# Delta-rule attention and a gated FFN on one core: the state product over two heads at once with a block-diagonal state, solve and within as stacked pairs of batch elements, and a new dealt order

## The chip, the cores and the metric

The kernel runs on one core of a Trainium2 chip. The metric is the device time of one execution in microseconds (us); the time shown for a kernel is the median of several runs. The names of the engines are those of the profile: PE (TensorE, matrix products; PEld are its weight loads), DVE (VectorE), ACT (ScalarE), POOL (GpSimd), SP (SyncE, which issues most DMAs).

## The reference

A delta-rule recurrence over 768 time steps for 4 batch elements and 8 heads of width 48, then a feed-forward layer with the gate h * cos(h). All data are 32-bit floats.

```python
k_n = k / (np.linalg.norm(k, axis=-1, keepdims=True) + 1e-06)
state = np.zeros((B, H, D, D))                       # B, H, S, D = 4, 8, 768, 48
for t in range(S):
    kt, vt, bt = k_n[:, :, t], v[:, :, t], beta[:, :, t, None]
    y[:, :, t] = np.einsum('bhd,bhde->bhe', q[:, :, t], state)
    v_old = np.einsum('bhde,bhd->bhe', state, kt)
    state = state + bt[:, :, :, None] * np.einsum('bhd,bhe->bhde', kt, vt - v_old)
x = y.transpose(0, 2, 1, 3).reshape(B * S, H * D)    # 3072 x 384
h = x @ w_in                                         # 384 x 2048
out = (h * np.cos(h)) @ w_out                        # 2048 x 384
```

## The kernel before

**Units.** Time is cut into 24 units of C = 32 steps. In a unit, 4 batch elements of 32 steps fill the 128 partitions: a quarter is 32 partitions (one batch element), a half is 64. Two units together are 256 tokens, one step of the feed-forward layer. Within a unit the recurrence is solved in closed form, by these stages (the numbers are lines of the kernel):

1. `turn` and `turn_out` (583 to 602), from unit 8 `load_blocks` and `turn_blocks` (356, 603): the keys and queries are transposed into kq_t, with the 48 features of an even head on partitions 0 to 47 and of an odd head on 64 to 111.
2. `gram` (609): for each of 4 head pairs j, 4 batch elements b and 2 parities `par` of the head a matmul of the keys with keys and queries, 48 rows, 32 columns of the array, 64 moving columns. `gram_keys` and `gram_queries` (627, 740) scale and mask the results on DVE.
3. The triangular inverse: units 0 to 3 by rows on PE, DVE and POOL (643 to 738); from unit 4 the gram goes to DRAM (`gram_put`, 749), comes back in another layout (`gram_get`, 764), is inverted on POOL column by column (`invert_eye` 774, `invert` 778: lines 791 and 798), and goes back through DRAM (`put` 800, `get` 806) into a tile zt.
4. `through_state` (816): keys (a = 0) and queries (a = 1) of the unit times the state, 64 matmuls of 48 rows, 32 columns of the array and 48 moving columns. The result p_kq lies in PSUM, batch elements on quarters, the parity of the head in the bank.
5. `right_side` (837, DVE): v less the keys' product. `solve` (882): the inverse times that, 32 matmuls of 32 by 32 with 48 moving columns; units 0 to 3 have two more products of that shape first (`solve_half`, `between`, by way of `triangular`, 850).
6. `solve_out` (895, DVE): weighs the result by beta and spreads it over two slots, one for each batch element of a half (the other slot is zero). `update` (908): 16 matmuls of 64 by 64 with 96 moving columns add to the state; `update_out` (920, DVE) adds them to the tile st.
7. `within` (926): the masked query gram times u adds to the queries' product in p_kq, 32 matmuls of 32 by 32, 48 columns. `within_out` (940, ACT) copies the sum to y, `features` (944) transposes y by three full transposes, `features_out` (954, ACT) copies the result into the features x of the feed-forward layer.

From unit 8 (PLAIN_TURNS) the odd heads are kept with the two halves of the partitions swapped: `home` (294) says in which quarter a batch element lies. The k loads (336), `gram`, `gram_put`, `weigh` (565), `spread_beta_home` (425), `solve`, `update` and `within` follow it.

**The feed-forward layer.** `hidden` (966) is a plain product for the first 256 tokens; later steps form the products by a scheme with 20 instead of 24 block products for the first layer (`layer`, 1145) and 7 instead of 8 for the second (`product`, 1225), with sums of operands on DVE and POOL. In between, ACT and DVE compute cos and the gate. The weights are loaded in 28 pieces (`narrows`, 458) and rewritten on ACT, DVE and POOL.

**The order.** Each stage is a task with dependences (`unit`, 1333). Which task is emitted when is written out by hand in one long list (`Order.LINE`), a table `Order.OTHER` names the tasks that run on their second engine or queue. Each engine works through its instructions in that order. So a stage that waits on PE holds all that PE has behind it. Buffers are counted in `Order.run`: PSUM has two banks for `p_kq`, two for `two` (turns, gram, solve, update, features), three for `h`, and one for the output.

Of the kernel before, what the change touches and what calls it, by code (L numbers as in the profile page):

```python
# [24 lines left out]
def _consts():  # L25

    p = np.arange(128)
    share = p // 64
    row = SPLIT * np.arange(C // SPLIT)[None, :] + share[:, None]
    return np.concatenate(
        [
            np.eye(128),
            p[:, None] % C < np.arange(C)[None, :],
            p[:, None] // C % 2 == np.arange(2)[None, :],
            p[:, None] // 16 % 2 == np.arange(2)[None, :],  # L40
            (row[:, :, None] == np.arange(C)).reshape(128, -1),
        ],
        axis=1,
    ).astype(np.float32)


class Order:

    OTHER = {
        ('weigh', 0, 0), ('fold', 0), ('unfold', 0), ('weigh', 0, 1), ('fold', 1), ('unfold', 1),  # L50
        ('fold', 2), ('fold', 3), ('unfold', 2), ('unfold', 3), ('in_sums', 6), ('in_sums', 8),
        ('in_sums', 14), ('in_sums', 15), ('x_sum', 2, 'd'), ('x_sum', 2, 'n'), ('x_sum', 2, 'm'),
        ('x_sum', 2, 'e'), ('x_sum', 2, 'k'), ('x_sum', 2, 'g'), ('x_sum', 2, 'i'),
        ('x_sum', 2, 'l'), ('x_sum', 2, 'f'), ('x_sum', 2, 'h'), ('x_sum', 2, 'b0'),
        ('left', 2, 1, 0), ('left', 2, 2, 0), ('left', 2, 3, 1), ('x_sum', 3, 'd'),
        ('x_sum', 3, 'n'), ('x_sum', 3, 'm'), ('x_sum', 3, 'e'), ('x_sum', 3, 'k'),
        ('x_sum', 3, 'g'), ('x_sum', 3, 'i'), ('x_sum', 3, 'l'), ('x_sum', 3, 'h'),
        ('x_sum', 3, 'b0'), ('left', 3, 1, 0), ('left', 3, 4, 0), ('x_sum', 4, 'd'),
        ('x_sum', 4, 'n'), ('x_sum', 4, 'm'), ('x_sum', 4, 'e'), ('x_sum', 4, 'k'),
        ('x_sum', 4, 'l'), ('x_sum', 4, 'f'), ('x_sum', 4, 'h'), ('x_sum', 4, 'b0'),  # L60
        ('left', 4, 4, 0), ('left', 4, 3, 0), ('left', 4, 3, 1), ('x_sum', 5, 'd'),
        ('x_sum', 5, 'n'), ('x_sum', 5, 'k'), ('x_sum', 5, 'g'), ('x_sum', 5, 'b0'),
        ('left', 5, 1, 1), ('left', 5, 4, 0), ('left', 5, 3, 0), ('left', 5, 3, 1),
        ('x_sum', 6, 'd'), ('x_sum', 6, 'n'), ('x_sum', 6, 'k'), ('x_sum', 6, 'g'),
        ('left', 6, 1, 0), ('left', 6, 2, 0), ('left', 6, 2, 1), ('left', 6, 4, 1),
        ('left', 6, 3, 0), ('x_sum', 7, 'd'), ('x_sum', 7, 'n'), ('x_sum', 7, 'm'),
        ('x_sum', 7, 'l'), ('x_sum', 7, 'h'), ('x_sum', 7, 'b0'), ('left', 7, 1, 0),
        ('left', 7, 3, 0), ('x_sum', 8, 'd'), ('x_sum', 8, 'n'), ('x_sum', 8, 'm'),
        ('x_sum', 8, 'g'), ('x_sum', 8, 'l'), ('x_sum', 8, 'h'), ('x_sum', 8, 'b0'),
        ('x_sum', 9, 'd'), ('x_sum', 9, 'f'), ('left', 9, 1, 0), ('left', 9, 2, 0),  # L70
        ('left', 9, 1, 1), ('left', 9, 4, 0), ('left', 9, 4, 1), ('left', 9, 3, 0),
        ('left', 9, 3, 1), ('x_sum', 10, 'd'), ('x_sum', 10, 'n'), ('x_sum', 10, 'm'),
        ('x_sum', 10, 'g'), ('x_sum', 10, 'i'), ('x_sum', 10, 'l'), ('x_sum', 10, 'b0'),
        ('left', 10, 1, 0), ('left', 10, 2, 1), ('left', 10, 3, 0), ('x_sum', 11, 'd'),
        ('x_sum', 11, 'n'), ('x_sum', 11, 'f'), ('x_sum', 11, 'h'), ('left', 11, 1, 0),
        ('left', 11, 4, 0), ('left', 11, 4, 1), ('left', 11, 3, 0), ('left', 11, 3, 1),
# [3 lines left out]
2031 0 1 9 10 2 3 15 16 17 11 54 55 18 56 57 21 4 60 22 23 19 58 61 62 6 24 25 26 27 28 30 34 63 64  # L80
29 93 92 101 65 66 32 102 31 2032 2035 2036 73 95 33 35 36 37 14 123 39 20 40 96 97 2037 2039 2038
124 2033 2034 38 132 133 69 2040 2041 41 67 42 43 44 2043 2044 45 2045 126 127 182 2047 2048 46 47
49 50 2049 2050 68 2042 128 2046 48 181 190 191 71 51 52 70 78 2051 53 98 2055 2056 2052 72 103 104
105 129 207 184 59 185 186 2053 2059 2060 94 2063 208 106 7 107 108 2067 238 2071 75 134 135 2054
739 74 137 138 2064 139 140 141 142 237 144 76 79 77 136 147 143 145 146 740 2075 2065 2061 80 81
82 263 83 148 2057 2068 2062 744 745 2058 741 742 100 84 85 2079 150 151 743 99 2076 86 87 149 2066
152 153 154 88 89 210 211 156 159 90 91 157 264 8 2083 293 240 5 12 109 2069 187 192 2077 193 194
2087 155 160 746 110 162 2072 2073 158 161 163 759 747 241 212 213 195 214 749 748 164 165 111 2084
2085 2080 2081 760 761 112 215 217 113 114 2078 2074 125 2070 2091 762 763 2088 166 2089 769 770
771 115 116 242 774 750 772 773 2082 216 2086 2090 218 117 119 243 244 219 775 776 777 751 778 120  # L90
2092 118 2095 2096 2099 2103 2093 764 246 247 2097 130 167 131 168 752 753 121 183 2107 2094 779
765 766 2100 122 767 220 221 2101 768 2098 2104 2105 209 189 2102 2108 2109 2106 2110 169 807 2111
170 171 172 13 808 822 823 824 173 809 810 174 811 222 2112 2113 2115 2119 319 817 2123 239 175 177
780 818 819 2127 791 176 2116 820 821 178 179 180 295 795 2117 2124 2125 796 265 812 813 814 266
2120 267 188 2131 827 2121 825 826 248 249 815 816 245 250 828 223 251 829 2114 2135 197 224 225
2132 2128 2129 2118 296 830 831 754 755 756 268 269 2136 2130 879 270 2126 2122 757 758 837 838 271
273 198 842 832 781 297 839 840 2139 2140 2133 2137 843 2134 2138 196 199 2141 2142 782 783 272 302
349 322 274 301 226 880 841 833 200 201 203 204 878 298 844 845 202 882 846 894 834 835 803 303 375
358 784 321 357 881 897 883 785 786 227 228 205 206 787 836 229 799 800 788 351 789 804 230 231 888
889 891 232 233 234 848 352 847 235 236 900 901 275 276 902 903 910 904 906 850 853 911 912 854 915  # L100
916 905 913 914 405 790 792 323 793 794 304 305 306 277 907 908 909 307 253 797 856 858 895 919 801
324 325 327 851 326 885 917 278 279 280 281 920 884 849 928 929 918 926 921 892 859 932 852 802 886
890 933 798 860 861 328 922 927 930 805 862 864 923 893 931 252 254 255 329 934 359 936 256 257 259
924 925 899 935 938 937 942 954 258 260 261 262 865 939 958 943 283 887 896 898 940 866 863 284 944
941 945 867 378 431 282 285 946 948 377 461 413 294 320 806 959 286 955 950 855 949 947 353 354 857
287 289 868 869 288 952 960 961 355 953 956 957 414 870 290 291 407 292 1014 330 331 1013 332 871
872 333 334 335 1015 1020 360 361 362 363 966 967 873 1024 1028 336 379 962 963 951 1016 1017 1019
1021 1018 874 875 876 350 380 381 383 309 1025 1026 964 982 968 969 965 985 1029 970 1030 408 978
979 1027 988 1032 299 1031 1039 1023 1033 971 1022 1041 300 310 382 972 973 983 1040 980 1034 337
385 1035 981 1036 1037 1042 1043 1044 984 989 991 993 1045 384 308 311 338 376 434 974 975 1046 312  # L110
487 1038 1047 1049 976 1048 1050 994 977 986 1051 1052 1071 987 1055 1056 313 315 314 995 1053 415
1057 316 339 317 318 992 1054 1072 996 997 433 990 340 435 470 877 490 517 341 342 1075 1058 1073
1074 999 1063 469 1001 343 345 344 1076 409 386 387 388 389 390 391 392 1002 346 1067 1061 1068 410
347 348 1062 1064 1126 1133 1003 416 417 418 406 419 1004 411 1059 1060 1065 1066 1128 1129 1127
998 1130 1131 1132 1136 1134 436 437 439 1000 1005 1006 1069 1137 1141 1007 1009 365 463 1070 393
1138 1091 1139 1010 464 465 1142 1143 438 1140 441 1144 1077 440 442 443 1135 1145 1146 364 1008
356 366 394 471 526 432 543 1078 1092 1011 1096 1152 1147 1153 1079 1080 367 368 1154 1081 1082
1093 1094 1156 1157 1155 1095 1148 1149 369 370 1150 371 372 1151 573 1083 1158 1159 1084 1098 373
1160 395 1087 1088 374 1101 1102 1089 1097 396 397 1162 462 1012 488 1161 1085 1164 398 399 401 402
489 525 599 1163 1168 466 1104 400 1086 1165 1166 1090 1106 1184 1099 1167 444 445 446 1169 403 404  # L120
# [95 lines left out]
def kernel(  # L216
# [73 lines left out]

    def home(n, b, par):
        return quarter(b ^ 2 if n >= PLAIN_TURNS and par else b)

    def by_parity(t):
        return t.rearrange("p (j a) i -> p a j i", a=2)

    bq = ffn_pool.tile([128, NU, C], FP, name="bq", tag="g", bufs=GATES)  # L300
    nc.vector.memset(bq, 0.0)

# [33 lines left out]
    def load(n, what="kqv", eng=(nc.sync,) * B):  # L336
# [4 lines left out]
        for x in what:  # L341
# [5 lines left out]
            if x == "k" and n >= PLAIN_TURNS:  # L347
                parts = [slice(0, H, 2), slice(1, H, 2)]
# [1457 lines left out]
```

## Time and profile before

| | |
|---|---|
| median of 3 runs | 651.01 us (650.0 to 652.37) |
| the profiled execution | 656.79 us, its span 654.2 us |
| mean granted clock of PE | 0.981 |
| PE busy | 619.1 us, 12306 matmul rows |
| DVE, ACT, POOL busy | 505.7, 265.5, 451.1 us |
| state (L828), all rows | 2944 in 23 units |
| solve (L891), update (L914), within (L931) | 1536, 736, 1536 rows |
| features (L950) | 72 rows |

The span is the time from the first to the last instruction; the execution's own time has 2.6 us around it. A row of PE is given with the rows and columns of the array that it uses (48*32), the shape of its moving operand (48x48), and how often it comes. Busy time overlaps where small matmuls run beside each other, so what a stage takes is read from the starts in the timeline.

### The profile page before, as it was taken

To read this page: it belongs to the slowest core of one execution; us is meant where nothing else is said; L and a number is where in the kernel's file an instruction comes from. 1 tells how busy PE (TensorE), PEld (TensorE's weight loads), DVE (VectorE), ACT (ScalarE), POOL (GpSimd) and SP (SyncE) were. 2 spreads that over 40 slices of the span, in tenths; PEclk is the share of its full clock that TensorE was granted. 3 is DMA by queue.
4 is the path that set the end of the run, shared out by engine and by line. 5 is a ranking of instruction groups with operands and counts; after the bars stand their busy time and mean duration, and the time that the engine had idled before them with its cause. 6 is when DMAs were issued, how large, how long until landed. Compare 5 with 4: busy or idle time off the path is not lost.

```text
span 654.2 us, 28227 instructions
## 1 busy us (share of the span) xinstructions
PE 619.1 (95%) x12306; PEld 579.8 (89%) x12306; DVE 505.7 (77%) x948; ACT 265.5 (41%) x469; POOL 451.1 (69%) x788
## 2 busy tenths in 40 slices
PE   5879799999999999998899999999999999999996
PEld 4778798976989999898799999999999999999996
DVE  7789798878999979776787877777777668667681
ACT  3545575731224523611542533622534523435340
POOL 3348989978988888686788986697787584143103
PEclk9979899999999999999799999999999999999999
DMA  7882573555444554434415434423400403000001
GB/s 157 192 217 72 130 217 82 118 107 75 90 68 67 115 73 71 95 67 81 77 29 93 67 62 77 90 40 62 85 7 13 105 4 60 13 2 25 2 13 36
DMA packets 202623, 49.99 MB, mean 76 GB/s; under 512 B 194244, under 2 KB 197460, under 8 KB 202500
## 3 DMA queue, kind: packets, MB, share of 16 engines
q1 hardware_dynamic: 201236, 47.81, 38.0%
q8 instruction: 96, 1.57, 1.0%
q10 hardware_dynamic: 1088, 0.20, 0.2%
q0 software_dynamic: 176, 0.18, 0.1%
q14 instruction: 27, 0.22, 0.1%
HBM read 38.19 MB, written 9.96 MB: 74 GB/s over the span
## 4 chain that ended last, share of the span: by engine, by line
PE 72%; POOL 8%; DVE 7%; DMA 6%; issue 3%; SPq 2%; ACT 2%; DVEq 0%; ACTq 0%; POOLq 0%
PE p_out L1229 23%; PE p_h L1149 23%; PE p_h L971 7%; PE p_out L1172 3%; DMA out_dram<-o 3%; PE p_kq L828 3%; PE p_u L891 2%; PE p_s L914 2%; POOL z L798 2%; POOL part L791 2%; PE p_kq L931 2%; PE p_g L619 2%; DVE turns L1019 1%; DMA qp<-in_q_dram 1%; PE p_z L950 1%
## 5 line engine op out<-in xcount | busy, mean ns | idle before, releaser
L791 POOL TENSOR_TENSOR part<-z,gb 128x126 f32<-128x126 f32 (+22 forms) x310 | 139.4, 450 | 56.2 <-DMA gb<-g_dr 15.7
L798 POOL TENSOR_TENSOR z<-z,part 128x126 f32<-128x126 f32 (+22 forms) x310 | 140.5, 453 | 24.4
L1229 PE MATMUL p_out<-w_out,g_ffn 128*128 128x192 f32 x672 | 122.5, 332 | 1.5 <-DVE o L1281 1.5
L1229 PEld LDWEIGHTS p_out<-w_out,g_ffn 128*128 128x128 f32 x672 | 109.0, 192 | 3.0 <-issue 1.1
L1028 ACT ACTIVATE turns<-turns,halfpi 128x512 f32<-128x512 f32 x96 | 68.7, 721 | 75.4 <-DVE turns L1019 74.8
L1229 PE MATMUL p_out<-w_sum,g_ffn 128*128 128x192 f32 x496 | 89.6, 329 | 1.8 <-DVE o L1281 1.8
L1245 POOL TENSOR_TENSOR g_ffn<-g_ffn 128x512 f32<-128x512 f32 x34 | 46.6, 1380 | 62.1 <-DVE g_ffn L1031 31.8
L1149 PE MATMUL p_h<-x_sum,w_in 128*128 128x128 f32 x640 | 84.8, 279 | 0.7 <-DVE g_ffn L1166 0.7
L1229 PEld LDWEIGHTS p_out<-w_sum,g_ffn 128*128 128x128 f32 x496 | 79.6, 191 | 2.9 <-DVE o L1281 2.2
L1149 PEld LDWEIGHTS p_h<-x_sum,w_in 128*128 128x128 f32 x640 | 78.7, 193 | 2.7 <-DVE g_ffn L1166 1.5
L1012 ACT ACTIVATE turns<-g_ffn,quarter_turn 128x512 int32<-128x512 f32 x70 | 50.0, 720 | 48.4 <-DVE g_ffn L1166 32.6
L1166 DVE TENSOR_TENSOR g_ffn<-g_ffn,p_h 128x512 f32<-128x512 f32 x80 | 54.2, 680 | 14.7 <-PE p_h L1149 12.1
L1019 DVE SCALAR_TENSOR_TENSOR turns<-g_ffn,turns 128x512 f32<-128x512 f32 x70 | 57.6, 831 | 8.6 <-ACT turns L1012 8.5
L1031 DVE TENSOR_TENSOR g_ffn<-turns,g_ffn 128x512 f32<-128x512 f32 x70 | 52.6, 758 | 12.7 <-ACT turns L1028 12.7
L1281 DVE SCALAR_TENSOR_TENSOR o<-p_out,o 128x192 f32<-128x192 f32 x74 | 25.1, 352 | 39.8 <-PE p_out L1229 29.7
L1149 PE MATMUL p_h<-x_sum,in_sum 128*128 128x128 f32 x400 | 54.2, 280 | 1.1 <-ACT p_h L1161 0.6
L971 PE MATMUL p_h<-x_ffn,w_in 128*128 128x128 f32 x384 | 50.4, 293 | 1.5 <-ACT row_copies L712 1.5
L1149 PEld LDWEIGHTS p_h<-x_sum,in_sum 128*128 128x128 f32 x400 | 49.2, 192 | 2.3 <-ACT p_h L1161 0.8
L971 PEld LDWEIGHTS p_h<-x_ffn,w_in 128*128 128x128 f32 x384 | 47.9, 206 | 2.5 <-ACT row_copies L712 1.6
L535 POOL TENSOR_TENSOR knrm<-ksum,halves 128x16 f32<-128x16 f32 (+1 forms) x14 | 37.0, 2646 | 15.7 <-DVE ksum L523 9.0
L1245 DVE TENSOR_TENSOR g_ffn<-g_ffn 128x512 f32<-128x512 f32 x54 | 42.5, 789 | 0.9 <-POOL part L791 0.3
L1149 PE MATMUL p_h<-x_ffn,w_in 128*128 128x128 f32 x320 | 42.8, 277 | 0.0
(144 smaller groups left out, 1041.5 us busy)
## 6 DMA issues: line engine op xcount, KB each, us to landing
gb<-g_dr SPq DMA_DIRECT2D x20, 256.0 KB
vp<-in_v_dram SPq DMA_DIRECT2D x96, 48.0 KB
in_sum<-in_moe_w_out_dram SPq DMA_DIRECT2D x12, 384.0 KB
out_dram<-o SPq DMA_DIRECT2D x23, 192.0 KB
in_sum<-in_moe_w_in_dram SPq DMA_DIRECT2D x8, 512.0 KB
kp<-in_k_dram SPq DMA_DIRECT2D x128, 24.0 KB
z_dr<-z SPq DMA_DIRECT2D x10, 256.0 KB
zt<-z_dr SPq DMA_DIRECT2D x80, 32.0 KB
```

Of the source, the lines that this page charges most:

```text
L535: nc.gpsimd.tensor_tensor(out=scales[m][2][:, part], in0=sums[m, part.start][:, 0:n], in1=halves[:, 0:n], op=ALU.pow,)
L791: nc.gpsimd.tensor_tensor(out=part, in0=z[:, 0:rows, j, None].to_broadcast(shape), in1=a[:, j, None, j + 1 :].to_broadcast(shape), op=ALU. ...
L798: nc.gpsimd.tensor_tensor(out=behind, in0=behind, in1=part, op=ALU.subtract)
L971: nc.tensor.matmul(p_h[:, i], w_in[:, t, (4 * k + i) * 128 : (4 * k + i + 1) * 128], xts[p][:, t, unit * 128 : (unit + 1) * 128], start=(i ...
L1012: nc.scalar.activation(turns[p, f], hidden_of(p, f), AF.Identity, bias=quarter_turn, scale=TURN)
L1019: nc.vector.scalar_tensor_tensor(out=r, in0=hidden_of(p, f), scalar=TURN, in1=t, op0=ALU.mult, op1=ALU.subtract,)
L1028: nc.scalar.activation(r, r, AF.Sin, bias=halfpi, scale=2.0 * math.pi)
L1031: nc.vector.tensor_tensor(out=place(p, f), in0=step_of(rests.pop((p, f)), f), in1=step_of(hidden_of(p, f), f), op=ALU.mult,)
L1149: nc.tensor.matmul(p_h[:, e], in_block(*w)[:, e], x_of(p, b), start=new and e == 0, stop=True, skip_group_check=True,)
L1166: nc.vector.tensor_tensor(out=part_of(p, to), in0=part_of(p, one), in1=part_of(p, two), op=op)
L1229: nc.tensor.matmul(p_o, left(p, part, a)[:, e % 4], right(e, b), start=(e == 0), stop=(e == FT // 2 - 1), skip_group_check=True,)
L1245: either(("left", p, x, s), nc.vector, nc.gpsimd).tensor_tensor(out=left(p, s, to), in0=left(p, s, one), in1=left(p, s, two), op=op)
```

## The change

The state is kept a second time as a tile st_wide, in which each pair of heads is a block-diagonal 128-row matrix (zero elsewhere); two copies a unit (`widen`, ACT or DVE) write the two diagonal blocks. A matmul of `through_state` then takes both heads of a pair: 128 rows, 32 columns, 96 moving columns, 32 matmuls in place of 64. zt becomes one tile that is set to zero once, with a batch element's inverse in its own slot, so that `solve` takes a half of the partitions at a time: 64 by 64, 48 moving columns, 16 matmuls in place of 32 (from unit 4). `within` takes a half of the rows and both slots of u: 16 matmuls with 96 columns. Its result has another layout (quarter 2*jh + i, slot x, then heads), `features` becomes 12 matmuls of 64 by 64 with the identity, and the rows of w_in are loaded to match, in two pieces each. The swapped quarters are gone, and with them the doubled k loads, the two extra puts, the copies in `weigh` and `spread_beta_home`; `weigh` may run on POOL in all units. There are three key buffers in place of four. The start of the inverse is written by three ACT copies of constants, and not copied from a constant loaded by DMA. `Order.LINE` and `Order.OTHER` are new throughout.

```diff
-    def home(n, b, par):
-        return quarter(b ^ 2 if n >= PLAIN_TURNS and par else b)
...
-    kps = [const.tile([128, 2, H, DP], FP, name=f"kp{i}") for i in range(4)]
+    kps = [const.tile([128, 2, H, DP], FP, name=f"kp{i}") for i in range(3)]
...
+    st_wide = const.tile([128, 2, NP, 2, 2, D], FP, name="st_wide")
+    wide_zt = const.tile([128, H, 2, C], FP, name="zt")
+    for t in [wide_zt, st_wide]:
+        nc.gpsimd.memset(t, 0.0)
...
     def invert_eye(m):
         zs[m] = work.tile([128, ROWS, C], FP, name="z", bufs=ZS)
-        nc.scalar.copy(zs[m], eye)
+        z = zs[m].rearrange("p r i -> p (r i)")
+        nc.scalar.copy(z, zero_one[:, 0:1].to_broadcast([128, ROWS * C]))
+        for i in range(SPLIT):
+            ones = z[half(i), i : ROWS * C : SPLIT * (ROWS + 1)]
+            nc.scalar.copy(ones, zero_one[half(i), 1:2].to_broadcast([DP, ROWS]))
...
     def get(n):
-        zts[n] = work.tile([128, H, C], FP, name="zt")
+        zts[n] = wide_zt
         z_dr = z_drs[n // 2].rearrange("r s u h b i -> u b (r s) h i")[n % 2]
         for b in range(B):
-            queue("get", n).dma_start(out=zts[n][quarter(b)], in_=z_dr[b])
+            queue("get", n).dma_start(out=zts[n][quarter(b), :, b % 2], in_=z_dr[b])
...
     def through_state(n):
...
         for a in range(2):
             for j in range(NP):
                 for b in range(B):
-                    for par in range(2):
-                        nc.tensor.matmul(
-                            p_kq[quarter(b), par, a, j],
-                            kq_t[rows48(par), a, b * NP + j],
-                            st[rows48(par), b // 2, j, b % 2],
...
+                    i, x = b // 2, b % 2
+                    if a == 0:
+                        to = p_kq[quarter(b), 0, 2 * j * D : 2 * (j + 1) * D]
+                        begin = j == 0
+                    else:
+                        at = (2 * x + j % 2) * 2 * D
+                        to = p_kq[quarter(2 * (j // 2) + i), 1, at : at + 2 * D]
+                        begin = j % 2 == 0 and x == 0
+                    nc.tensor.matmul(
+                        to,
+                        kq_t[:, a, b * NP + j],
+                        st_wide[:, i, j, x].rearrange("p q e -> p (q e)"),
...
     def solve(n):
...
+                for i in range(2):
                     nc.tensor.matmul(
-                        p_u[home(n, b, par), par, j], zt[quarter(b), h], rhs[quarter(b), h]
+                        p_u[half(i), par, j],
+                        zt[half(i), h].rearrange("p x i -> p (x i)"),
+                        rhs[half(i), h],
                     )
...
+    def widen(n, par):
+        to = st_wide[half(par), :, :, :, par].rearrange("p i j x e -> p (i j x) e")
+        by = st[half(par)].rearrange("p i j x e -> p (i j x) e")
+        if ("widen", n, par) in Order.OTHER:
+            nc.vector.tensor_copy(to, by)
+        else:
+            nc.scalar.copy(to, by)
...
     def within(n):
         u, tt, p_kq = us.pop(n), grams.pop(n), p_kqs[n]
...
+        for jl in range(2):
             for par in range(2):
+                for jh in range(2):
+                    for i in range(2):
+                        h = 2 * (2 * jh + jl) + par
+                        at = (2 * jl + par) * D
+                        nc.tensor.matmul(
+                            out_at[quarter(2 * jh + i), :, at : at + D],
+                            tt[half(i), h],
+                            u[half(i), h],
...
     def features(n):
...
-        for t in range(KT):
-            nc.tensor.transpose(p_z[:, t], y_f[:, t * 128 : (t + 1) * 128], ident)
+        for k in range(KT):
+            for x in range(2):
+                for jh in range(2):
+                    nc.tensor.matmul(
+                        p_z[half(jh), k, x],
+                        y[half(jh), x, k * DP : (k + 1) * DP],
+                        ident[half(jh), half(jh)],
...
-            add(("get", n), "SP", 1.9, lambda: get(n), [("put", m)],
+            add(("get", n), "SP", 1.9, lambda: get(n),
+                [("put", m)] + ([("solve", n - 1)] if n > 2 * ROWED else []),
...
+        state = [("widen", n - 1, i) for i in range(2)]
         add(("state", n), "PE", 1.17 if n else 0.0, lambda: through_state(n),
-            [("gram", n), ("update_out", n - 1)] if n else [("gram_queries", 1)],
+            [("gram", n)] + state if n else [("gram_queries", 1)],
```

## The prediction

> **What bounds the kernel now.** I read the page's busy rows first, then its chain of work that ended last, then who PE waited for, then PE's timeline around three units of the recurrence.
>
> ```profile
> PE 619.1 (95%) x12306; PEld 579.8 (89%) x12306; DVE 505.7 (77%) x948; ACT 265.5 (41%) x469; POOL 451.1 (69%) x788
> PE 72%; POOL 8%; DVE 7%; DMA 6%; issue 3%; SPq 2%; ACT 2%; DVEq 0%; ACTq 0%; POOLq 0%
> ```
>
> PE is busy 95% of the span and carries 72% of the chain; no other engine is over 77%. The waits listed for PE add up to some 30 us, over half of it in the first 75 us; the largest later piece is 4.8 us before the solve at 313.6 us. So, after the first 75 us, what a stage takes on PE is what the end pays. The next lines show these stages (start, time to the modelled end of the last one, count). I take as a stage's cost the distance from its start to the start of the next row, since the modelled ends overlap.
>
> ```profile
> 321.52 1.47 PE L1229 MATMUL p_out<-w_out,g_ffn 128*128 128x192 f32 x8
> 322.82 1.05 PE L1149 MATMUL p_h<-x_sum,w_in 128*128 128x128 f32 x8
> 323.81 1.38 PE L828 MATMUL p_kq<-st,kq_t 48*32 48x48 f32 x128
> 325.12 1.16 PE L1149 MATMUL p_h<-x_sum,in_sum 128*128 128x128 f32 x8
> 326.11 0.49 PE L950 MATMUL p_z<-consts,y 128*128 128x128 f32 x3
> 326.44 1.05 PE L1149 MATMUL p_h<-x_sum,in_sum 128*128 128x128 f32 x8
> 327.33 1.06 PE L1149 MATMUL p_h<-x_ffn,w_in 128*128 128x128 f32 x8
> 328.32 0.80 PE L891 MATMUL p_u<-rhs,zt 32*32 32x48 f32 x64
> 329.05 1.16 PE L1149 MATMUL p_h<-x_ffn,in_sum 128*128 128x128 f32 x8
> 330.04 1.06 PE L1149 MATMUL p_h<-x_sum,w_in 128*128 128x128 f32 x8
> 331.03 0.89 PE L914 MATMUL p_s<-u,kp 64*64 64x96 f32 x32
> 331.85 0.80 PE L931 MATMUL p_kq<-u,tt 32*32 32x48 f32 x64
> 332.58 1.16 PE L1149 MATMUL p_h<-x_sum,in_sum 128*128 128x128 f32 x8
> ```
>
> State 1.31 us, features 0.33, solve 0.73, update 0.82, within 0.73. A matmul is two rows of the trace (32 matmuls of solve are x64), I call a row a pass; a transpose is one. In the large stages a pass of 192 columns costs 1.30/8 = 0.163 us and one of 128 columns 0.89/8 = 0.111: it goes by its columns. By that, 96 columns are 0.081, 64 are 0.056, 48 are 0.041. Small matmuls run beside each other. Unit 2 shows it, from the time before the quarters were swapped:
>
> ```profile
> 81.58 0.88 PE L858 MATMUL p_v<-u_half,halves_z 32*32 32x48 f32 x64 [0.60 <-ACT u_half L868]
> 82.39 2.95 PE L971 MATMUL p_h<-x_ffn,w_in 128*128 128x128 f32 x24
> 85.27 0.88 PE L891 MATMUL p_u<-u_half,halves_z 32*32 32x48 f32 x64
> 86.08 2.95 PE L971 MATMUL p_h<-x_ffn,w_in 128*128 128x128 f32 x24
> ```
>
> Here a batch's rows meet the same quarter of columns, four places in the array, 64/4 = 16 passes each: 16 x 0.041 = 0.66, measured 0.81, so 0.15 is start and drain. Update has four places (two halves by two halves), 8 passes each: 8 x 0.081 = 0.65, measured 0.82, so 0.17. Both fit one rule: **passes per place x columns, plus 0.16 us**; the number of instructions (64 and 32) doesn't enter. From unit 8 on, the swapped quarters give solve and within eight places, and both fall from 0.81 to 0.73.
>
> **The change on PE, stage by stage.**
> - Solve, units 4 to 23: 16 matmuls of 64 by 64, 48 columns, 32 passes on only two places (half to same half): 16 x 0.041 + 0.16 = 0.82. Half the instructions, no gain: +0.09 in 16 units (8 to 23), nothing in 4 to 7. **+1.4 us.**
> - Within: 16 matmuls, 96 columns, 32 passes on four places: 8 x 0.081 + 0.16 = 0.81, as update. +0.08 in 16 units. **+1.3 us.**
> - Features: three transposes of full size (three passes, 0.33) become 12 matmuls with the identity, 24 passes of 64 columns, on two places (half jh to half jh): 12 x 0.056 + 0.16 = 0.83. **+0.50 x 24 = +12.0 us.** No row shows a 64-column matmul of this kind; from below, 24 passes at the rate per pass of today's state (1.31/128 = 0.010) would be 0.25, from above one after the other 24 x 0.056 + 0.16 = 1.5. I take 0.83, by the update row, which is nearest in shape.
> - State, 23 units: 64 matmuls on eight places become 32 with all 128 rows, 32 columns of array and 96 moving columns: 64 passes on four places, the column quarters. If all four always run, 16 x 0.081 + 0.16 = 1.46. But the query half (a = 1) writes quarters 2(j//2)+i: pairs j = 0, 1 use quarters 0 and 1 alone, j = 2, 3 quarters 2 and 3. Then it is 8 passes deep for the keys and 8 + 8 for the queries: 24 x 0.081 + 0.16 = 2.10. The far ends: 64 passes at 0.010 give 0.65; one after the other they take 64 x 0.081 + 0.16 = 5.3. That quarters sharing their rows run together is shown by today's state (two halves of rows, four quarters on each: 64 passes of 0.041 on each half would be 2.6 us in turn, and it takes 1.31). How far PE reaches past a blocked quarter is shown by these two lines, a gram followed at once by a state:
>
> ```profile
> 290.81 0.22 PE L828 MATMUL p_kq<-st,kq_t 48*32 48x48 f32 x1
> 290.82 0.27 PE L619 MATMUL p_g<-kq_t 48*32 48x64 f32 x4
> ```
>
> One pass of state starts ahead of gram's last four, so it reaches some four passes; to start quarters 2 and 3 early it would have to reach past 16. I take 2.10: +0.79 x 23 = **+18.2 us**, and keep 1.46 and 5.3. The Trainium skill, "TensorE: Matmul & The Clock Gate", Part 3 (The mechanism), says that matmuls start in strict program order and only weight loads are pulled ahead. By that rule the state would be near the 2.10 too; the two lines above show that it isn't quite strict here.
> - Gram: as it was, 0.79 alone. Where a state is its neighbour (12 places by the order of before) they share a shape and gram costs 0.58 (290.23 to 290.81); the new state has another shape. **+0.2 x 12 = +2.4 us.**
>
> Sum on PE: 1.4 + 1.3 + 12.0 + 18.2 + 2.4 = +35.3 us. Units 0 to 3 run before 95 us, where PE is idle for some 18 us of the first 100; their share (3 x 0.79 + 4 x 0.50 = 4.4) I count by half: **+33 us**.
>
> **What lies beside PE.** Widen copies 64 rows of 768 elements twice a unit (29 on ACT, 17 on DVE). ACT's square of 128x768 takes 0.84 us, its copy of 128x512 0.62, DVE's add of 128x768 0.95. So ACT gets 29 x 0.84 = 24 us more at 41% busy; DVE gets up to 16 and loses 24 copies of some 0.24 and, with weigh moved to POOL, 7 times 0.96. Neither becomes the bound. But widen is a new wait of state, and behind state all of PE is queued. Today the shortest time from the end of the sum to state is 1.8 us. In the new order at least 3.4 us of PE work (by the costs above) stands between the start of update and the next state, but for one early unit with 2.0; update 0.82, sum 0.95, and one or two widens (0.84 or 1.7) with hand-overs of 0.1 to 0.2 make 2.8 to 3.7. So I cost it at nothing beyond 1 to 2 us; with that cover gone it is at most one widen a unit, 23 x 0.84 = 19 us. The single zt buffer lets get start only after solve of the unit before; 10 us of PE work or more lie between two solves, and four gets take 2.1 us of SP to issue. The fewer DMAs (k loads 8 to 4 a unit, puts 3 to 1; weights 12 more) relieve SP, which isn't late on PE's rows except once. The two more ACT copies of invert's start, the memsets and kps 4 to 3 are hidden behind the same slack. The order dealt anew may save or add some of the 30 us of waits: 0 taken, 8 either way.
>
> So the profiled execution (656.8 us, span 654.2) would become 690; the median of the runs shown, 651.0, lies 5.8 lower, and I forecast 651 + 33 = **684 us**.
>
> **Rivals.**
> 1. All four quarters run in the query half: state 1.46, sum 20.6, less 2: 651 + 18.5 = 670 us. For: in update all four places work at once. Against: the query half names only two quarters for 16 passes. It decides where PE reaches 16 passes ahead. Chance 0.32.
> 2. **Faster: cost goes by the number of instructions.** If every pass costs the 0.010 of today's state, state is 0.65 (-15 us), solve and within 0.33 (-18), features 0.25 (-2): 651 - 35 = 616. It decides where the pass is shorter than the issue of the places' passes in turn; for: eight places hardly beat four (0.73 against 0.81). Against: update's 32 passes last as long as p_v's 64. Chance 0.07. The Trainium skill, "TensorEngine Tiling (Array Packing)", Instruction Overhead, gives each matmul some 60 cycles whatever its width, which would favour the change; by it, at the 2.4 GHz in the first table of its "TensorE: Matmul & The Clock Gate", today's state of 128 passes would need an estimated 3.2 us, and the trace has 1.31.
> 3. The widen becomes the wait: 684 + up to 19 = 703. The order speaks against it. 0.08.
> 4. Quarters with shared rows don't run together: state 5.3, 684 + 74 = 758. 0.04.
>
> **How the numbers follow.** The forecast has 0.44, rival 1 0.32, 2 0.07, 3 0.08, 4 0.04; the rest (0.05) is an order that wins or loses more than 8, 0.02 of it faster and 0.03 no change. The range takes the forecast and rival 1 with 8 us of order on the low side and part of rival 3: 662 to 699. A measurement tells 0.3% from no change: faster 0.09, same 0.03, slower 0.88.
>
> **What would show it.** State's row at 2.1 (forecast), 1.46 (rival 1) or 0.65; features at 0.83; solve and within both near 0.82 from unit 8 on; PE's busy time up by some 30 us with idle time as before. Features still at 0.33 or state under 1.3 would make it wrong.

## The result and the profile after

The changed kernel takes **677.38 us** (median of 4 runs, 676.89 to 677.82) against 650.5 us for the kernel before (4 runs, 647.96 to 652.37). The ratio is 1.0416, 95% interval 1.0378 to 1.0453: 27 us slower. The profiled execution took 677.82 us, its span is 676.0 us.

The busy row of PE and the chain of the work that ended last, from the page of the kernel after:

```profile
PE 644.7 (95%) x9930; PEld 601.4 (89%) x9930; DVE 500.4 (74%) x937; ACT 293.6 (43%) x514; POOL 456.5 (68%) x796
PE 85%; DVE 4%; DMA 3%; POOL 2%; ACT 2%; SPq 2%; issue 1%; POOLq 0%; ACTq 0%; DVEq 0%
```

PE has 2376 rows fewer and is busy 25.6 us longer, and it now carries 85% of the chain. PE's timeline of the kernel after, around three units (start, time to the modelled end, engine, line, operation, count):

```profile
301.68 1.93 PE L820 MATMUL p_kq<-st_wide,kq_t 128*32 128x96 f32 x64
303.54 0.86 PE L608 MATMUL p_g<-kq_t 48*32 48x64 f32 x64
304.33 0.92 PE L1249 MATMUL p_out<-w_sum,g_ffn 128*128 128x192 f32 x4
```

```profile
318.09 1.13 PE L889 MATMUL p_u<-rhs,zt 64*64 64x48 f32 x32
319.15 1.57 PE L1249 MATMUL p_out<-w_out,g_ffn 128*128 128x192 f32 x8
320.65 0.89 PE L914 MATMUL p_s<-u,kp 64*64 64x96 f32 x32
321.47 0.86 PE L944 MATMUL p_kq<-u,tt 64*32 64x96 f32 x32
322.26 2.87 PE L1249 MATMUL p_out<-w_out,g_ffn 128*128 128x192 f32 x16
324.97 1.05 PE L1169 MATMUL p_h<-x_sum,w_in 128*128 128x128 f32 x8
325.95 0.92 PE L965 MATMUL p_z<-consts,y 64*64 64x64 f32 x24
326.80 1.93 PE L820 MATMUL p_kq<-st_wide,kq_t 128*32 128x96 f32 x64
328.66 1.16 PE L1169 MATMUL p_h<-x_sum,w_in 128*128 128x128 f32 x8
```

From each start to the next: state 1.86 us (before 1.31), gram 0.79, solve 1.06 (0.73), update 0.82, within 0.79 (0.73), features 0.85 (0.33). Every stage that the change gives a new shape has grown.

| what PE spends, from starts to next starts over the whole span | before | after |
|---|---|---|
| state | 29.6 us | 43.5 us |
| features | 8.8 | 22.6 |
| solve | 21.1 | 26.7 |
| within | 19.7 | 20.9 |
| gram, update | 40.1 | 39.1 |
| the products of the feed-forward layer, with the waits that follow them | 478.4 | 464.9 |
| early stages (rows, triangles, turns) | 46.7 | 48.1 |

The stages of the recurrence cost 33.5 us more, the early ones 1.4 more, and the products 13.5 less. The products are the same instructions in both kernels, so what they lost is waits and slow clock: PE's waits after the first 100 us are 12.2 us before and 3.4 after. Part of the 13.5 belongs to the profiled execution of before, which at 656.79 us is longer than the median: in a second profile of that kernel (experiment 7) the products take 473.5 us, 8.6 more than after.

### The profile page after: what moved, and what is told of

Its sections match the earlier page's. It is cut to its first block, busy times and chain, and to the rows that moved or that the text cites. A ratio compares the mean times of both kernels' runs of the same rounds, so it can differ in the third digit from the quotient of the medians.

```text
span 676.0 us, 23446 instructions
## 1 busy us (share of the span) xinstructions
PE 644.7 (95%) x9930; PEld 601.4 (89%) x9930; DVE 500.4 (74%) x937; ACT 293.6 (43%) x514; POOL 456.5 (68%) x796
## 4 chain that ended last, share of the span: by engine, by line
PE 85%; DVE 4%; DMA 3%; POOL 2%; ACT 2%; SPq 2%; issue 1%; POOLq 0%; ACTq 0%; DVEq 0%
PE p_out L1249 27%; PE p_h L1169 27%; PE p_kq L820 6%; PE p_h L991 6%; PE p_u L889 3%; PE p_out L1192 3%; PE p_s L914 3%; PE p_z L965 3%; PE p_kq L944 3%; PE p_g L608 2%; DMA qp<-in_q_dram 1%; SPq L348 1%; DVE turns L1039 1%; PE p_o L1249 1%; POOL w_in L502 1%
## 5 line engine op out<-in xcount | busy, mean ns | idle before, releaser
L1265 POOL TENSOR_TENSOR g_ffn<-g_ffn 128x512 f32<-128x512 f32 x36 | 48.6, 1361 | 80.1 <-DVE g_ffn L1051 36.9
L1039 DVE SCALAR_TENSOR_TENSOR turns<-g_ffn,turns 128x512 f32<-128x512 f32 x70 | 58.3, 839 | 12.9 <-ACT turns L1032 12.7
L991 PE MATMUL p_h<-x_ffn,w_in 128*128 128x128 f32 x384 | 47.4, 281 | 0.2 <-ACT row_copies L701 0.2
L1181 ACT COPY p_h<-p_h 128x512 f32<-128x512 f32 x40 | 22.9, 573 | 54.8 <-PE p_h L1169 50.9
L991 PEld LDWEIGHTS p_h<-x_ffn,w_in 128*128 128x128 f32 x384 | 44.9, 195 | 1.6 <-ACT row_copies L701 0.4
L820 PE MATMUL p_kq<-st_wide,kq_t 128*32 128x96 f32 x1472 | 44.3, 249 | 0.2 <-ACT st_wide L933 0.2
```

What stands on the lines that cost most here:

```text
L820: nc.tensor.matmul(to, kq_t[:, a, b * NP + j], st_wide[:, i, j, x].rearrange("p q e -> p (q e)"), start=begin, stop=(a == 0), skip_group_c ...
L991: nc.tensor.matmul(p_h[:, i], w_in[:, t, (4 * k + i) * 128 : (4 * k + i + 1) * 128], xts[p][:, t, unit * 128 : (unit + 1) * 128], start=(i ...
L1039: nc.vector.scalar_tensor_tensor(out=r, in0=hidden_of(p, f), scalar=TURN, in1=t, op0=ALU.mult, op1=ALU.subtract,)
L1265: either(("left", p, x, s), nc.vector, nc.gpsimd).tensor_tensor(out=left(p, s, to), in0=left(p, s, one), in1=left(p, s, two), op=op)
```

## The experiments

Each kernel is the changed one with the edit shown, where nothing else is said; ratios are to the kernel before.

**1. The queries' quarters in turn.** The order of the 16 query matmuls of the state product, so that neighbours go to different quarters; the work is the same.

```diff
-            for j in range(NP):
-                for b in range(B):
+            for s in range(NP * B):
+                    if a == 0:
+                        j, b = s // B, s % B
+                    else:
+                        j, b = 2 * (s // 2 % 2) + s // 8, 2 * (s % 2) + s // 4 % 2
```

> The changed kernel, with only the query half of the state product put in another order, so that successive matmuls go to quarters 0, 1, 2, 3 in turn, as the key half does. Theory (the query half keeps only two quarters busy): state falls from 1.86 us to 16 x 0.081 + 0.16 = 1.46, 23 x 0.40 = 9 us less, 677.4 to some 668. Rival (with all 128 rows in every matmul the loads of 32 columns go in turn, 64 x 0.028 = 1.8 us): state stays at 1.86 and the time at 677.

671.24 us, ratio 1.0262 (1.0189 to 1.0335). The timeline of this kernel:

```profile
300.83 1.53 PE L823 MATMUL p_kq<-st_wide,kq_t 128*32 128x96 f32 x64
302.29 0.86 PE L608 MATMUL p_g<-kq_t 48*32 48x64 f32 x64
```

State is 302.29 - 300.83 = 1.46, the price of four quarters that always run. So order alone makes the 0.40 us between 1.86 and 1.46. That is 9.2 us in 23 units, and the time falls by 6.1, to between the 668 of the theory and the 677 of the rival; the row of the stage decides for the theory. Both kernels have the same count of PE rows: row for row, this one is 2.2 us late at 98 us and 5.7 us early at the end. The 7.9 us between are 0.40 in each of the 20 units left, so after the start all of it arrives.

**2. Solve by quarters** from unit 4: 32 matmuls of 32 by 32 again, over the same zt.

```diff
-                for i in range(2):
+                for b in range(B):
                     nc.tensor.matmul(
-                        p_u[half(i), par, j],
-                        zt[half(i), h].rearrange("p x i -> p (x i)"),
-                        rhs[half(i), h],
+                        p_u[quarter(b), par, j], zt[quarter(b), h, b % 2], rhs[quarter(b), h]
                     )
```

> The changed kernel, with solve from unit 4 on as 32 matmuls of 32 by 32 again (a batch element's own quarter, four places), and not 16 of 64 by 64. Theory (a pass takes the longer of its moving columns and of the columns that its weight load fills: 64 of these are 0.056 us, 48 moving ones 0.041): solve falls from 1.06 us to 16 x 0.041 + 0.16 = 0.82, 20 x 0.24 = 5 us less, some 672.5. Rival (the order's slack takes it up, or double the instructions cost as much): no change, 677.

672.73 us, ratio 1.0288 (1.0227 to 1.0349): 4.65 us back. Solve takes 0.81 here with twice the instructions.

**3. Features by two full transposes and four small matmuls** (the first 256 features of y whole, the last 128 by halves, the rows of w_in loaded to match).

```diff
-        for k in range(KT):
...
+        for x in range(2):
+            nc.tensor.transpose(
+                flat.rearrange("p (k i x t) -> p x (k i) t", k=KT, x=2, t=C)[:, x, 0:4],
+                y[:, x, 0:128],
+                ident,
+            )
+        for x in range(2):
+            for jh in range(2):
+                nc.tensor.matmul(
+                    p_z[half(jh), 2, x],
...
```

> The changed kernel, with features as two full transposes (columns 0 to 127 of each slot) and four 64 by 64 matmuls with the identity, in place of twelve of these; the rows of w_in are loaded to match. Theory: 2 x 0.111 + 4 x 0.056 + 0.16 = 0.61 in place of 0.84, 24 x 0.23 = 5.5 us less, some 672. Rival (a change of shape within the stage costs another 0.15 to 0.2): 0.8, 676.5.

673.64 us, ratio 1.0293 (1.0227 to 1.036): 3.7 us back, less than expected. Its timeline says why:

```profile
325.11 0.38 PE L965 MATMUL p_z<-consts,y 128*128 128x128 f32 x2
325.42 0.45 PE L972 MATMUL p_z<-consts,y 64*64 64x64 f32 x8
325.80 1.93 PE L822 MATMUL p_kq<-st_wide,kq_t 128*32 128x96 f32 x64
```

0.31 + 0.38 = 0.69: the two kinds each pay a start, so a stage gains only 0.85 - 0.69 = 0.16, which is 3.8 us in 24 units.

**4. The three together.**

> The three edits together: query quarters in turn, solve by quarters, features mixed. Theory (PE's time alone sets the end, so the three add up): 9 + 5 + 5.5 = 19.5 us less than 677.4, some 658, that is a ratio of 1.01 to the kernel before. Rival (waits for other engines take the place of PE's work as it shrinks): above 664.

659.82 us (10 runs), ratio 1.0109 (1.0072 to 1.0146): 17.6 us back, near the 658 of the theory. The parts alone gave 6.1 + 4.65 + 3.7 = 14.5. The 3 us between come from the start, which differs between executions: from the update of unit 4 (at 141 us in the changed kernel) to the end of the span the traces have 7.5, 4.9 and 4.4 us less for the parts, 16.8 together, and 15.4 for this kernel.

**5. Solve with 24 columns.** Half of the moving columns of solve are left out (the result is used twice), so that its passes move 24 columns and not 48.

```diff
-                        p_u[half(i), par, j],
+                        p_u[half(i), par, j, 0 : D // 2],
...
-                        rhs[half(i), h],
+                        rhs[half(i), h, 0 : D // 2],
```

> The changed kernel, with solve from unit 4 on over 24 of the 48 moving columns; the other 24 columns of the result are filled with a copy of the first. So half of solve's product is left out. Theory (the load of 64 columns bounds the pass, 0.056 us): solve stays at 1.06 us. Rival (a pass is its moving columns and a fixed 0.015): 16 x (0.020 + 0.015) + 0.16 = 0.72.

676.65 us (one run). Its timeline:

```profile
317.22 1.11 PE L889 MATMUL p_u<-rhs,zt 64*64 64x24 f32 x32
318.26 1.57 PE L1252 MATMUL p_out<-w_out,g_ffn 128*128 128x192 f32 x8
```

1.04 us with half the moving columns, 1.06 with all: not they, but the weights, 64 columns for each pass, set solve's time.

**6. No widen.** The copies into st_wide are left out after unit 0, so the state product reads old values.

```diff
+        if n:
+            return
```

> The changed kernel, without the copies of the state into its block-diagonal form after unit 0: the state product multiplies by the state of unit 0 ever after, and doesn't wait for the sum. Theory (widen is covered): 0 to 2 us less than 677.4. Rival 3 of the prediction (widen is the wait): up to 19 us less, 658.

677.82 us (677.12 to 678.45), ratio 1.0417 (1.0351 to 1.0483): no change. In the kernel after the list of what PE waited for has the widen once:

```profile
PE p_kq L820 <- ACT st_wide L933: 0.2, 1, 0.2
```

**7. The kernel before once more**, without an edit, for how much its waits differ between executions.

> The kernel before, unchanged, profiled once more. Theory (the wait of 4.8 us before the solve at 313.6 us in its profile, and the half-speed clock behind it, belong to that execution, which took 656.8 us against a median of 650.5): a span near 648 without such a wait. Rival (the wait is of the order before, and the dealt order took it away): the wait is there again, span near 654.

653.29 us, span 651.5, between the 648 of the theory and the 654 of the rival. The 4.8 us ahead of the solve at 313.6 us, the longest late wait of the first profile, aren't in its list; the waits after 100 us are 9.0 us (12.2 in the first). So some 3 us of those waits belonged to one execution.

**8. Natural queries.** The block-diagonal state is kept, with its new order. The queries' product goes to a batch element's own quarter again, so solve and within are 32 by 32 and features three full transposes.

```diff
-                    if a == 0:
-                        to = p_kq[quarter(b), 0, 2 * j * D : 2 * (j + 1) * D]
...
+                    to = p_kq[quarter(b), a, 2 * j * D : 2 * (j + 1) * D]
+                    begin = j == 0
```

> The changed kernel and its order, with the block-diagonal state product kept, but the queries' product written to a batch element's own quarter, as the keys' is. Then solve and within are 32 matmuls of 32 by 32 again, features three full transposes, and the rows of w_in are loaded as before. Theory (PE's stages set the end): state 1.46, solve and within 0.81, features 0.33; against the changed kernel 23 x 0.40 + 20 x 0.25 + 24 x 0.52 = 27 us less on PE, of which the single edits gave back a third of the state's part: 650 to 654. Rival (as PE shrinks, waits take its place): 658 or more.

654.03 us (12 runs), ratio 1.0026 (0.9998 to 1.0054) to 652.55 in 17 runs of before: no difference that can be told, at the upper edge of the 650 to 654 expected. Its state takes 1.46, solve and within 0.81, as expected. It is the best version of this study, and it doesn't beat before.

**9. The order alone.** Kernel 8 with the narrow state product of before (64 matmuls a unit, no widen).

```diff
-                        st_wide[:, i, j, x].rearrange("p q e -> p (q e)"),
+                    for par in range(2):
...
+                            st[rows48(par), b // 2, j, b % 2],
```

> As the last one, with the state product of before too (64 matmuls of 48 rows, no block-diagonal copy): what is left of the change is the order dealt anew, the quarters not swapped, three key buffers and the work beside PE. Theory (the dealt order has 6 to 9 us fewer waits after 100 us than that of before, and the rest of the change costs PE): state 1.31, solve and within 0.81, so PE's stages are 16 x 2 x 0.08 = 2.6 us dearer than before, and the time is 644 to 648, under before. Rival (the dealt order waits less only because PE has more to do in it): 650 to 654, no gain on before.

679.72 us (674.07 to 689.54), ratio 1.0407 (1.0361 to 1.0453). I had expected 644 to 648: a miss by 33 us. The profiled execution was the slowest, 689.54 us. The first lines of its list of PE's waits, and its timeline:

```profile
PE p_g L605 <- issue: 13.1, 6, 3.9
PE p_kq L812 <- issue: 9.2, 6, 2.3
```

```profile
315.35 1.38 PE L812 MATMUL p_kq<-st,kq_t 48*32 48x48 f32 x128
316.55 0.70 PE L605 MATMUL p_g<-kq_t 48*32 48x64 f32 x46
319.29 0.38 PE L605 MATMUL p_g<-kq_t 48*32 48x64 f32 x18 [2.04 <-issue]
```

With the smaller lines PE waits 27 us for "issue", for nothing that the profile names, and in the midst of a stage: 46 rows of gram, 2 us of nothing, the other 18. It looked as if PE ran out of instructions, here behind 128 + 46 = 174 small rows.

**10 and 11. Gram and state kept apart.** In kernels 9 and 8 one or two products of the feed-forward layer (1.8 to 2.7 us) are put between each gram and the state beside it (17 numbers moved in the list of the order): the trace of kernel 9 has ten stretches of gram and state without a break, that of kernel 10 has one.

> The kernel of the run before (the dealt order, the state product of before, quarters not swapped), with only the order of some tasks changed: wherever a gram and a state follow each other on PE, one or two products of the feed-forward layer (1.8 to 2.7 us) are moved between them. Theory (PE runs dry of instructions: there its trace shows 27 us of waits for nothing but issue, most of them in the middle of a gram or state behind some 190 small matmuls in a row): these waits mostly go, and the time falls by 18 to 28 us, from 679.7 to 652 to 662. Rival (the waits come from the state product itself or its data, not from what stands beside it): 670 or more.

> The same moves in the order, in the kernel with the block-diagonal state product and natural queries (654.0 us, 5 us of waits for issue). Theory: it has half the matmuls in the state and rarely ran dry, so little changes: 650 to 655. Rival (moving the feed-forward products is good or bad by itself): a change of 5 us or more either way.

Kernel 10 takes 663.92 us, ratio 1.0182 (1.0138 to 1.0227), and 8.6 us of "issue" are left in its list. Kernel 11 takes 660.21 us, ratio 1.0124 (1.0082 to 1.0165), 6.2 us more than kernel 8, where I had expected next to none: there the rival holds, the moves cost something by themselves. Kernel 10 is 15.8 us faster than kernel 9, 2 us short of the 652 to 662 expected. If the moves cost the same 6.2 us in it, which no run shows, they took 22 us of the dryness off.

**12. The kernel before, moved by 64 rows.** The part of the DMA queues has a row for instructions, on the page of the kernel before:

```profile
q8 instruction: 96, 1.57, 1.0%
```

1.57 MB in 96 packets are 16 KB each. The 12306 rows and their 12306 weight loads over 96 give 256 instructions, so a packet feeds 128 rows. In the trace of kernel 9 these packets never begin less than 3.4 us apart. The eleven places after the first 100 us at which more than 1 us lies between the starts of two neighbouring rows are the rows 1994, 2630, 3521, 4413, 5304, 5814, 6324, 7217, 8237, 10149 and 10658: distances of 5, 7, 7, 7, 4, 4, 7, 8, 15 and 4 times 127.2 to 127.6 rows. So these waits fall on the ends of packets. In nine of the eleven the 127 rows ahead had run in 1.2 to 1.7 us. If that is the cause, the time hangs on where the ends fall, and the kernel before should have the fault too as soon as its ends are moved:

```diff
+            if n == 0 and a == 1:
+                for _ in range(8):
+                    for b in range(B):
+                        nc.tensor.matmul(
+                            p_t[quarter(b), 1, 0, 0:C],
+                            ident[quarter(b), quarter(b)],
+                            ident[quarter(b), 0:C],
+                        )
```

> The kernel before, with 32 matmuls of 32 by 32 (64 rows) more at the very start, in a wait of 1.4 us that PE has there for the first queries; they compute nothing that is kept. They cost under 1 us themselves, and they move every later instruction of PE by 64 rows against the pieces in which PE's instructions are fetched (96 pieces and 12306 rows in the kernel before: 128 rows and their 128 weight loads to a piece). Theory: PE runs dry at the end of a piece whose 128 rows it gets through in well under some 3.2 us (the shortest that such pieces took in the dealt order with the narrow state), so the time depends on where the pieces' ends fall among the small matmuls. Laid over the starts in the trace of the kernel before, ends as they were give 0 to 1 us of such waits, ends moved by 64 rows 11 or 12 waits of over 0.9 us, 23 us together, as many as the order alone had; with what the clock loses after each, 670 to 690 us, ratio 1.03 to 1.06, waits named issue in gram (L619) and state (L828). Rival: the waits of the order alone were due to its order, and not to the pieces: 650 to 655 us, ratio 1.00, issue waits under 3 us as before.

680.52 us (676.35 to 682.81, 6 runs), ratio 1.0414 (1.0377 to 1.045): 32 tiny matmuls at the start cost 28 us. Its waits of PE, its timeline, and its windows (stretch; length, PE busy and rows; granted clock; DMA share; GB/s):

```profile
PE p_kq L836 <- issue: 15.5, 10, 2.5
PE p_g L627 <- issue: 10.5, 4, 3.4
```

```profile
304.80 1.15 PE L836 MATMUL p_kq<-st,kq_t 48*32 48x48 f32 x101
307.88 0.39 PE L836 MATMUL p_kq<-st,kq_t 48*32 48x48 f32 x26 [1.93 <-issue]
```

```profile
305.90:307.88 1.98, 0.05 (x4) 1.00 0.50 60
307.88:309.88 2.00, 2.00 (x32) 0.64 0.58 82
309.88:311.88 2.00, 2.00 (x10) 0.50 0.13 21
311.88:314.00 2.12, 2.12 (x17) 1.00 0.45 75
```

The state product stops after 102 of its 128 rows (101 here and one that starts among the rows of gram ahead). Of the rows at which the long waits end, 1994, 2630, 3521 and 6324 are the same numbers as in kernel 9 with its other order, and the other six (4538, 7342, 8360, 9379, 10399, 11671) lie whole multiples of 127.1 to 127.6 rows from them: it is the count of instructions that decides. And most stops are paid twice: behind seven of the eight waits of 1.9 to 2.5 us after the first 100 us, the granted clock is 0.5 for some 3.4 us.

## Why the prediction was right, and where it wasn't

The forecast of 684 us (662 to 699) holds 677.38, and the sign is right. By its own steps:

- **What bounds the kernel:** right. PE's stage costs rose by 34.0 us by its way of counting (state 0.55 x 23 = 12.7, features 12.2, solve 0.33 x 16 + 0.25 x 4 = 6.3, within 1.0, gram 1.8), against 35.3 forecast, and no other engine became the bound.
- **Features 0.83, within 0.81, gram 0.79:** measured 0.85, 0.79, 0.79. Only the gain that gram loses beside a state was counted a little too high: a gram and a state together took 1.94 us before (290.23 to 292.17), which is 0.16 less than 0.79 + 1.31, in 11 places, and after 2.65 (301.68 to 304.33), which is no less than the two apart. The rule of passes per place x columns + 0.16 us carried over to shapes that the trace of before didn't have.
- **State, 2.10 us:** measured 1.86, so the term of 18.2 us was 12.7. The step that failed is "it reaches some four passes". Experiment 1 shows the mechanism, quarters left idle by the order of the queries, and its size, 0.40 and not 0.64. In the starts of a state from 301.68 us the queries begin two by two every 0.083 us; at 302.73, when six of the first sixteen haven't begun, two more join in each step, and after four such steps only these go on. The trace doesn't name the quarters; that the late ones are the other two is read from the counts. The Trainium skill, "TensorE: Matmul & The Clock Gate", Part 3 (The mechanism), has the matmuls start in strict order; by that rule the state would be near 2.10. The trace doesn't agree.
- **Solve, 0.82 us:** measured 1.06, so 1.4 us were 6.3. The step that failed is that a pass goes "by its columns", by the moving ones. Experiment 5 halves these and nothing moves; experiment 2 halves the loaded ones and 0.25 us go. 16 passes of 64 loaded columns are 16 x 0.056 + 0.16 = 1.06. Loaded rows don't count: in experiment 1 passes of 128 rows, 32 loaded and 96 moving columns fit 0.081 us. So a pass costs the larger of the columns it moves and of those it loads. The Trainium skill, same page, "LDWEIGHTS (loading the stationary operand)", has a load go by its columns, P / 1.2 ns, which for 64 is an estimated 53 ns; the 0.056 agrees. The prediction could have read this in the trace of before, in the row products of the early units, whose six passes here load 128 columns and move 24, 16 and 8, two of each:

```profile
43.06 0.83 PE L701 MATMUL p_r<-rows,w_sum 128*128 128x24 f32 x6
```

The six starts lie 0.11 us apart, at a granted clock of 1.00: the price of 128 columns, and not the 0.02 of 24.

- **Widen costed at nothing:** right, by experiment 6; rival 3 falls. **Rival 1** (all four quarters run) holds only once the order is changed, in experiment 1. **Rival 4** (5.3 us) falls with the 1.86. **Rival 2** (cost by the number of instructions) falls for what a stage takes; but there is a cost that goes by the number, below.
- **The order dealt anew, taken at 0, and the early units, counted by half:** of the 34.0 us, 34.0 - 26.9 = 7.1 don't arrive. PE's waits after 100 us fall from 12.2 us (9.0 in the second profile) to 3.4, while those of the first 100 us rise from 18 or 19 to 23. How much of the 7.1 is order, how much lighter queues and how much the early units isn't separated; experiment 9, which was to show the order alone, met a fault of its own.

Two errors of 5 us, state too dear and solve too cheap, cancelled: that is luck. What didn't arrive of the sum made the rest of the distance to 684. The sum was nearer to the truth than its terms.

What the prediction missed altogether is that the time of before rests on luck. I laid packets of 127.4 rows, each to last at least 3.2 us, over the starts in the traces, at 16 offsets 8 rows apart. That is a model, with its floor taken from kernel 9. After the first 100 us it gives before 0.1 to 23.4 us of waits, and under 1 where its ends in fact lie; the kernel after at most 2.9 at any offset, and kernel 8 at most 1.9. So, by the model, the halved state product takes away a risk that the kernel before happens not to meet; experiment 12 shows that risk, 28 us, for before. For the block-diagonal form the runs agree as far as they go: kernels 2, 3, 4, 8 and 11 each have another count of rows or another order, and so other ends, and none has more than 2.1 us of waits for issue after the first 100 us. Against before as it stands, that is worth nothing.

## What to carry to other kernels

Fewer, larger matmuls in the array are no gain by themselves: count the passes at the busiest place, take for each the larger of moved and loaded columns, and add one start per stage and shape. Put neighbouring matmuls on different places; the order of a loop alone was worth 0.40 of 1.86 us. Where over a hundred small matmul rows follow each other, an edit anywhere ahead of them can cost or gain some per cent by moving the ends of the instruction packets: test such a kernel with a few idle matmuls put in front before a difference is laid to the edit.

## What the runs showed of the hardware that I had not expected

- **PE can run out of instructions.** A packet of 16 KB feeds 128 rows, and none began less than 3.4 us after the last (kernel 9; before 3.43), while 128 rows of the narrow state product run in 1.3 us. In kernel 9 the packet that ends a long wait had begun 2.3 to 2.9 us ahead of its first row. PE is never more than about one packet ahead: in the trace of before, when PE passes the end of a packet, no packet beyond the one that it enters has begun in 71 of 95 places, and only one more in the other 24. So slow work ahead of a fast stretch lays little by. The Trainium skill, "Runtime: NRT & Kernel Launch", Instruction fetch mechanics, has the blocks of 16 KB and 256 instructions, and the trace agrees; that the fetch is hidden behind the issue of instructions isn't so here, 26 us of waits in kernel 12.
- **A wait of 2 us can be enough for the clock to fall** to 0.5 for some 3.4 us (the windows of kernel 12), so that it costs nearly twice its length. It isn't always: kernel 12 has one wait of 2.05 us (ahead of 357.32 us) with the clock at 1.00 behind it, and in kernel 9 the clock fell after one of 1.51 us (ahead of 227.26 us) and not after one of 2.29 (ahead of 188.87 us).
- **A pass with 64 loaded columns takes 0.056 us** whether it moves 24 or 48 (1.04 and 1.06 us of solve).
